# Making the low parts of the expert weights on VectorE instead of GpSimd

## The chip, the cores and the metric

One core of a Trainium2 chip runs the whole program. The metric is the device time of one execution in microseconds (us); the time before is the median of 3 runs.

## The reference, cut to what matters

Attention over 4 x 8 heads gives 2304 rows of 512 features; a gated MLP with RMS norm follows; then the part that matters here, a mixture of 8 experts with a fixed capacity:

```python
cap = N // E                                  # 2304 / 8 = 288
logits = x @ w_gate
order = np.argsort(-logits.flatten())
for idx in order:                             # greedy, best pair of token and expert first
    tok, e = (int(idx) // E, int(idx) % E)
    if assigned[tok] >= 0 or counts[e] >= cap:
        continue
    assigned[tok] = e
    counts[e] += 1
for e in range(E):
    mask = assigned == e
    h = np.maximum(x[mask] @ w1[e], 0.0)      # 288x512 by 512x1024
    out[mask] = h @ w2[e]                     # 288x1024 by 1024x512
```

## The kernel before, in words

The first 880 us are attention and the gated MLP, which the change does not touch. The rest is the function `routed`.

**Products.** Every fp32 operand is kept as a high part, rounded to the format that TensorE multiplies at full rate, and a low part, the difference. A product is three matmuls (`mm3`, lines 1029 to 1033): high by high, high by low, low by high. An expert has 16 units of 12 matmuls, each with 288 columns: `ffn1` eight times (one block of 128 hidden features each), then `ffn2` eight times (four output blocks, two halves each). After a unit, ScalarE takes the high part out of PSUM (lines 1044, 1023) and VectorE the low part (lines 1045, 1024). Four transposes at the start bring an expert's gathered tokens into place (`xpose`), four at the end turn its outputs (`turn`), and GpSimd's indirect DMAs gather and scatter the rows.

**Weights.** An expert's weights come in 8 slots of 128x1024 (512 KB each), loaded by SyncE's queue as soon as the expert is known and one of 8 buffers is free (`load`, `weights`). `split` (lines 1007 to 1013) makes of a slot the two parts: ScalarE copies it into the high part `wh`, and GpSimd subtracts that from the slot, which gives the low part `wl`. A slot serves two units. `cut` emits the splits so that they are LOOK = 4 slots ahead of the unit that is being emitted.

**Routing.** It closes one expert per phase. In a phase (`propose`, `search`, `close`) VectorE finds each token's best open expert (lines 788 to 798), and a search in six steps finds the threshold: VectorE makes candidates (`ci`, line 834), compares all tokens with them (`g`, line 801, two comparisons of half of the tokens each), TensorE counts with 18 small matmuls (line 807), VectorE tests the counts (`sat`, line 853), one matmul spreads the result (line 856) and VectorE scans it (line 861). Then come prefix sums (line 897 and the matmuls of lines 908 and 909) and a chain of 18-column operations. `tokens` turns the result into row numbers (the table `hb`, line 965; 18 matmuls, line 977) and starts the gather. Phase 0 runs before the first expert's products, the others beside the products; phase r + 1 starts only when the tokens of expert r - 1 are transposed (the loop on `turned` in `phases`, line 1105).

**Order of the work.** Every engine runs its instructions in the order in which they are emitted, and that order is laid out by hand. Two clocks are kept while emitting: `now` for TensorE and `vec` for VectorE. After each matmul of a product, `aside` adds 0.12 us to `now` and emits the operations of the routing whose time has come by these clocks. A flow hands over the cost of its next operation on either engine before it goes on. VectorE work that has some time is put in the list `late` by `evac`, with a weight (0.37 us by default) and a due time WAIT = 0.8 us after `now`. It leaves the list first in, first out, when it is due or when it fits ahead of the routing's next operation (by up to FIT = 0.4 us), and then `vec` is advanced by its weight; `settle` empties the list as far as a tag demands. `ffn1` and `ffn2` call `settle` with the slot's tag `(r, s)` before they use a slot (lines 1038 and 1052); in the kernel before, nothing in the list carries such a tag. GpSimd's subtraction is emitted directly after ScalarE's copy and is in neither clock.

Of the kernel before, what the change touches and what calls it, by code (L numbers as in the profile page):

```python
# [38 lines left out]
def body(tc, kq, vv, tab, w64, rg, wg2, w1, w2, ident_d, tri_d, jtab_d, cand_d, itab_d, out, dbg=None):  # L39
# [11 lines left out]
    wg2_t = cst.tile([128, 4, NE], F32, name="wg2_t")  # L51
    # the identity between the router's blocks (hi and lo, hi beside it)
    WI = cst.tile([128, 2, 160], F32R, name="WI")
# [4 lines left out]

    # ------------------------------------------------------------------ attention and MoE 1
    st = ExitStack()  # L60
# [72 lines left out]
    def rope_mul(n):  # L133
        """k and q turned: x cos + (x swapped) sin."""
        dve.tensor_mul(X[n][:, 0], X[n][:, 0], tab_t[:, 0])
        pool.tensor_mul(X[n][:, 1], X[n][:, 1], tab_t[:, 1])
# [30 lines left out]
    def v_scale(n):  # L167
        """A power of two that brings the head's V into the range of the halves."""
        p = VA.pop(n)
        sc = IS[n] = wa.tile([128, 3], I32, name="sc", bufs=3)  # L170
        dve.tensor_scalar(sc[:, 0:1], p[:, 0:1].bitcast(I32), 0x7F800000, None, op0=ALU.bitwise_and)
        dve.tensor_scalar(sc[:, 2:3], sc[:, 0:1], float(27 << 23), float(-(14 << 23)), op0=ALU.max, op1=ALU.add)
        dve.tensor_scalar(sc[:, 1:2], sc[:, 2:3], -1.0, float(254 << 23), op0=ALU.mult, op1=ALU.add)
# [107 lines left out]
    def step(u):  # L281
        """One step: scores of tile u, maxima of a tile ahead, the product with V of a tile behind,
        and its share of what the heads around need. Each engine finds its operands made a step or
        more before, so that none holds up another."""
        n, kt = divmod(u, KT)
# [78 lines left out]

    # ---- RMS norm and the transposed input
    def prep(b):
# [7 lines left out]
        def stats():  # L374
            """The squares of the last head; those of the others are there."""
            dve.tensor_scalar(m, m, 1.0 / DM, 1e-6, op0=ALU.mult, op1=ALU.add)
            for t in range(KT):
                squares(t, DM - D, DM, c)
# [39 lines left out]

    # ---- weights of MoE 1 in slots of 4 blocks
    NSLOT = 2 * NF + 12  # L420
# [4 lines left out]
    def w_ahead(to):  # L425
        """Loads the slots up to one, which there is room for."""
        while w_next[0] <= to and w_next[0] < B * NSLOT:
            n = w_next[0]
            w_next[0] += 1
            if n < NSLOT:  # L430
                if n < 2 * NF and n % 3 == 2:
                    WR[n] = flat[:, 0:1024].bitcast(I32).rearrange("p (k c w) -> p k c w", k=4, w=2)
                else:
                    WR[n] = wk.tile([128, 4, 128, 2], I32, name="w8")
                sp.dma_start(WR[n], w64[n].bitcast(I32))
            else:
                WR[n] = wk.tile([128, 4, 128], F32, name="wr" if n % 2 else "w8")
                sp.dma_start(WR[n], ws[n % NSLOT])
# [4 lines left out]
    def w_turn(g):  # L443
        """Queues the making of float32 words from the bits of slot g, and their store for later use."""
        if g >= NSLOT:
# [24 lines left out]
    def w_split(g):  # L470
        """Queues what brings slot g in its two parts, and the words of the slot after the next."""
        if g >= B * NSLOT:
# [33 lines left out]
    def pump():  # L506
        """Splits the slots that take the room of those used up to the unit before."""
        while used and used[0][0] < unit[0]:
            w_split(used.pop(0)[1] + NW)
        unit[0] += 1  # L510
        drain(2 if queue and queue[0][0] < NSLOT else 3)
# [32 lines left out]
    def logits(b, d, hf):  # L544
        """A block of features: turned into rows, and its part of the router's logits beside."""
        xh, xl = XT.pop((b, d, hf))
        j = 2 * (b % 2) + hf
        t0 = b // 2 * 9
        p = psB.tile([128, 512], F32, name="pb")
        # the last 32 rows go to partitions 32 j on, behind rows that nobody reads  # L550
        cut = [(0, 0, 128), (1, 128, 128), (2, 256 - 32 * j, 32 * j + 32)]
# [160 lines left out]
def routed(tc, top, t1, w1, w2, tri_d, jtab_d, cand_d, itab_d, out):  # L712
    """Each phase closes one expert: the one whose CAP-th best proposal is the best of such. A
    token proposes to the open expert it likes best; the expert closed takes its CAP best
    proposals, and the others propose anew."""
    nc = tc.nc
# [31 lines left out]
    dve.memset(taken, BIG)  # L748
    # row 8 of a satisfied table is 1: lift's product is 2^120 or more where an expert is
    # satisfied, -2^120 elsewhere  # L750
    lift = c2.tile([NE + 1, 128], BF16, name="lift")
    dve.tensor_scalar(lift, itab[0:NE + 1, 30:31].to_broadcast([NE + 1, 128]), 2.0 ** 120, None, op0=ALU.mult)
    # the sum of the marks of the satisfied experts
    marks = c2.tile([NE + 1, 128], BF16, name="marks")
# [16 lines left out]

    # The routing is written as flows: before each of its operations it hands over what that
    # will cost on the tensor and on the vector engine (us), and goes on when its time has come.

    HT = NT // 2

    # a token's proposal: v its value, wm the mark of the expert, 2^(8 - expert)
    def propose(r, lo=0, hi=NT):
# [33 lines left out]
    def early():  # L812
        """Half of the first phase's first step."""
        for _ in propose(0, 0, HT):
            pass
        g, p = R[0]["first"] = grid()
        compare(0, g, cand0, 0, 64)
        yield
        count(0, g, p, 0, 64)

    def search(r):
        """The largest value that some expert has CAP proposals at or above, a few bits at a
        time; the candidates are in falling order."""
        z = R[r]
        v = z["v"]
        o = 0
        for s, (_, bits) in enumerate(STEPS):
# [34 lines left out]
            fp = y[:, n - 1:n]  # L862
        # of the experts that have them, the first
        f = z["f"] = wk.tile([128, 2, NT], BF16, name="f")
# [11 lines left out]
    def last(r):  # L876
        """The expert that is left takes the tokens that are left."""
        z = R[r]
# [7 lines left out]
    def close(r):  # L886
# [25 lines left out]
        yield 0, 0.08  # L912
        # how many of those at the threshold there is room for
        dve.tensor_scalar(k[:, 2:3], q[:, 0, NT:], -1.0, float(CAP), op0=ALU.mult, op1=ALU.add)
# [26 lines left out]
    def tokens(r):  # L941
        """From a closed expert to its tokens' rows."""
        z = R.pop(r)
# [14 lines left out]
        dve.scalar_tensor_tensor(bb, ai, float(-GT), pos, op0=ALU.mult, op1=ALU.add)  # L958
        # two tiles side by side: 16-bit pairs go through at twice the rate
        hb = wk.tile([128, HT, GT, 2], BF16, name="hb")  # L960
# [26 lines left out]
        if r == 0:  # L987
            # the rest of the first weights comes behind these rows
            e = wk.tile([1, 1], I32, name="ev2")
            pool.tensor_copy(e, evs[0])  # L990
            sv[0] = sp.value_load(e, min_val=0, max_val=NE - 1)
            held.clear()
            load()
# [13 lines left out]
    def split(r, s):  # L1007
# [3 lines left out]
        act.activation(h, t, AF.Copy)  # L1011
        pool.tensor_sub(l, t, h.bitcast(F32))  # L1012
        ws[r, s] = (h, l)
# [69 lines left out]

    # The order of the emission: the experts' products one after the other, and between them,
    # when its operands are about to be there, the next operation of the routing; for that, the
    # clocks of the two engines are kept as they will run.
    now, vec = [1.1], [0.0]
# [23 lines left out]
    def hum(t):  # L1111
        """The array would fall back to half its clock while nothing but the routing runs."""
        while cold and t - now[0] > 0.4:
# [41 lines left out]
    def evac(tag, f, w=0.37):  # L1155
        """A vector operation that has some time."""
        late.append((now[0] + WAIT, w, f, tag))
# [7 lines left out]
    def settle(tag, keep=0):  # L1165
        """No more than the last few of a kind are still to come."""
        while sum(x[3] == tag for x in late) > keep:
            flush(1)

    def load():  # L1170
        """Weights of known experts, as far as there is room."""
        while loads and loads[0][0] in known and len(loads) > len(splits) - 8 and loads[0][1] not in held:
# [48 lines left out]
def rows():  # L1221
    """The row of each place of the router's tiles: of the half of a batch two tiles of 128 and a
    quarter of the ninth."""
    p, t = np.arange(128)[:, None], np.arange(NT)[None]
# [75 lines left out]
```

## Time and profile before

| what | value |
|---|---|
| time, median of 3 runs (lowest, highest) | 1280.33 us (1279.73, 1283.87) |
| span of the profiled execution (its only own time) | 1273.8 us |
| TensorE, VectorE, ScalarE, GpSimd busy | 1112.7, 803.8, 601.2, 772.9 us |
| mean granted TensorE clock | 0.939 |

The span runs from the first to the last instruction of one execution that the profiler recorded; a run's time is some 6.5 us longer. In the rows, PE is TensorE, PEld its weight loads, DVE VectorE, ACT ScalarE, POOL GpSimd, SP SyncE. A line reads: line of the kernel, engine, operation, output<-inputs, shapes. In a timeline the first two numbers are start and duration in us, and brackets hold the engine's idle time ahead of the instruction and what ended it.

### The profile page before, as it was taken

Reading aid. Unit: us, or ns where it says so; the run is one execution under the profiler, and the core shown is the slowest. Engines: PE = TensorE matmul, PEld = TensorE weight load, DVE = VectorE, ACT = ScalarE, POOL = GpSimd, SP = SyncE. Lnnn points to the kernel's source line nnn. Section 1 sums busy time; section 2 is a strip of 40 time slices with the busy share of each in tenths; the row PEclk is TensorE's granted clock in tenths of the full one; section 3 lists DMA queues with packets and bytes.
Section 4 is the critical chain, followed back from the end, with each engine's and each line's share of the span. In section 5 each row is a group of like instructions: output and inputs, shape, how many; then the busy total and the mean of one; then the engine's idle time right before and its main releaser. Section 6 shows DMA issues by size and latency. Waiting matters only on the chain.

```text
span 1273.8 us, 25985 instructions
## 1 busy us (share of the span) xinstructions
PE 1112.7 (87%) x9973; PEld 1033.8 (81%) x9973; DVE 803.8 (63%) x1825; ACT 601.2 (47%) x1387; POOL 772.9 (61%) x623
## 2 busy tenths in 40 slices
PE   3677789888979999888999999999888778988997
PEld 2666678787979999878999999997477767777996
DVE  6799889889885566456655343222776778567320
ACT  3566755445555656455665554432032233233552
POOL 4687678888546888534776526641254454455874
PEclk9897798999999999888999999999998889799999
DMA  5766446556653536334341223220322433343531
GB/s 167 190 179 176 129 139 201 192 160 179 192 152 107 155 94 176 81 97 135 93 127 57 78 80 105 84 81 25 114 105 103 152 130 92 103 129 115 178 112 32
DMA packets 73196, 159.04 MB, mean 125 GB/s; under 512 B 8976, under 2 KB 22960, under 8 KB 73072
## 3 DMA queue, kind: packets, MB, share of 16 engines
q1 hardware_dynamic: 70000, 147.94, 38.9%
q0 software_dynamic: 3072, 9.44, 2.5%
q8 instruction: 78, 1.28, 0.4%
q14 instruction: 46, 0.38, 0.1%
HBM read 110.52 MB, written 18.87 MB: 102 GB/s over the span
## 4 chain that ended last, share of the span: by engine, by line
PE 57%; DVE 26%; issue 5%; DMA 4%; ACT 3%; POOL 3%; SPq 1%; another core or an unknown queue 0%; POOLq 0%; DVEq 0%; ACTq 0%
PE psf L1032 13%; PE pb L500 9%; PE pb L501 9%; PE pb L502 9%; DVE mx L215 3%; DVE wr L459 2%; PE pss L807 2%; PE pa L190 2%; PE pa L208 2%; DVE wr L455 2%; DVE ci L834 2%; DMA QQ<-X 2%; PE pa L191 2%; DVE g L801 2%; DVE L L571 1%
## 5 line engine op out<-in xcount | busy, mean ns | idle before, releaser
L500 PE MATMUL pb<-XH,wh 128*128 128x288 f32 x768 | 230.2, 300 | 1.9 <-DVE t L532 1.9
L501 PE MATMUL pb<-XL,wh 128*128 128x288 f32 x768 | 229.4, 299 | 0.0
L502 PE MATMUL pb<-XH,wl 128*128 128x288 f32 x768 | 229.4, 299 | 0.0
L1012 POOL TENSOR_TENSOR wl<-rw,wh 128x1024 fp32r<-128x1024 f32 x64 | 153.5, 2410 | 104.2 <-ACT wh L1011 101.8
L202 POOL TENSOR_TENSOR PL<-pe,PH 128x576 f16<-128x576 f32 x136 | 189.2, 1396 | 37.4 <-ACT PH L199 26.8
L196 ACT ACTIVATE pe<-pa 128x288 f32<-128x288 f32 x320 | 121.7, 409 | 126.2 <-PE pa L191 118.5
L482 POOL TENSOR_TENSOR wl<-wr,wh 128x512 fp32r<-128x512 f32 x90 | 118.8, 1320 | 98.5 <-ACT wh L481 98.2
L500 PEld LDWEIGHTS pb<-XH,wh 128*128 128x128 f32 x768 | 147.8, 192 | 2.2 <-DVE t L532 2.1
L501 PEld LDWEIGHTS pb<-XL,wh 128*128 128x128 f32 x768 | 147.4, 192 | 0.0
L502 PEld LDWEIGHTS pb<-XH,wl 128*128 128x128 f32 x768 | 147.2, 192 | 0.0
L538 POOL TENSOR_TENSOR HL<-q,HH 128x288 fp32r<-128x288 f32 x96 | 87.2, 909 | 85.1 <-ACT HH L537 80.3
L190 PE MATMUL pa<-QQ,KK 128*128 128x288 f32 x320 | 107.9, 338 | 13.1 <-DVE mx L215 10.1
L500 PE MATMUL pb<-HH,wh 128*128 128x288 f32 x384 | 117.0, 305 | 0.7 <-DVE XL L402 0.5
L208 PE MATMUL pa<-KK,QQ 128*128 128x288 f32 x230 | 83.3, 362 | 36.9 <-ACT pe L196 22.3
L502 PE MATMUL pb<-HH,wl 128*128 128x288 f32 x384 | 114.3, 298 | 1.3 <-POOL wl L482 1.3
L501 PE MATMUL pb<-HL,wh 128*128 128x288 f32 x384 | 114.2, 297 | 0.0
L215 DVE TENSOR_REDUCE mx<-pa 128x1 f32<-128x288 f32 x230 | 101.3, 449 | 13.2 <-PE pa L208 12.8
L199 ACT ACTIVATE PH<-pe 128x576 f16<-128x576 f32 x160 | 108.8, 680 | 0.0
L532 DVE SCALAR_TENSOR_TENSOR t<-t,pb 128x288 f32<-128x288 f32 x96 | 43.5, 453 | 102.5 <-ACT t L531 101.8
L191 PE MATMUL pa<-QQ,KK 128*128 128x288 f32 x320 | 101.5, 318 | 1.8 <-DMA QQ<-mt 1.8
L482 POOL TENSOR_TENSOR wl<-w,wh 128x512 fp32r<-128x512 f32 x54 | 69.8, 1293 | 45.0 <-ACT wh L481 44.9
L481 ACT ACTIVATE wh<-wr 128x512 fp32r<-128x512 f32 x90 | 56.3, 625 | 72.0 <-DVE wr L459 65.8
(209 smaller groups left out, 3350.1 us busy)
## 6 DMA issues: line engine op xcount, KB each, us to landing
rw<-w SPq DMA_DIRECT2D x64, 512.0 KB
X<-kq SPq DMA_DIRECT2D x31, 576.0 KB
w<-w SPq DMA_DIRECT2D x28, 512.0 KB
w<-ws SPq DMA_DIRECT2D x54, 256.0 KB
wr<-ws SPq DMA_DIRECT2D x54, 256.0 KB
ws<-wr SPq DMA_DIRECT2D x36, 256.0 KB
KK<-X SPq DMA_DIRECT2D x31, 288.0 KB
QQ<-X SPq DMA_DIRECT2D x31, 288.0 KB
```

The costliest lines, as they stand in the source:

```text
L190: pe.matmul(p[:, 0:HS], BK[i][:, ks], AQ[i][:, qs], start=True, stop=False)
L191: pe.matmul(p[:, 0:HS], FK[i][:, ks], EQ[i][:, qs], start=False, stop=True)
L196: act.activation(E[u][:, h * HS:(h + 1) * HS], SM.pop((u, h))[:, 0:HS], AF.Exp, scale=1.0 / math.sqrt(D))
L199: act.activation(PH[u % NP][:, 0:S], E[u], AF.Copy)
L202: eng.tensor_sub(PL[u % NP][:, 0:S], E.pop(u), PH[u % NP][:, 0:S])
L215: dve.tensor_reduce(MX[n][:, qt, h:h + 1], XM.pop((u, h))[:, 0:HS], axis=AX.X, op=ALU.max)
L482: pool.tensor_sub(l, r, h.bitcast(F32))
L500: pe.matmul(p, wh[:, k], xh, start=first, stop=False)
L501: pe.matmul(p, wh[:, k], xl, start=False, stop=False)
L502: pe.matmul(p, wl[:, k], xh, start=False, stop=last)
L1012: pool.tensor_sub(l, t, h.bitcast(F32))
L1032: pe.matmul(p, a[:, k], b, start=first and i == 0, stop=last and i == 2)
```

## The change

In `split`, the subtraction that makes `wl` goes from GpSimd to VectorE, and from direct emission into the list `late`, with the tag `(r, s)` and the weight 1.13 us. It holds for all 64 slots. The rest of the diff takes comments and docstrings out.

```diff
@@ -1009,7 +1009,7 @@
         h = wb.tile([128, 8, 128], F32R, name="wh", bufs=8)
         l = wb.tile([128, 8, 128], F32R, name="wl", bufs=8)
         act.activation(h, t, AF.Copy)
-        pool.tensor_sub(l, t, h.bitcast(F32))
+        evac((r, s), lambda: dve.tensor_sub(l, t, h.bitcast(F32)), 1.13)
         ws[r, s] = (h, l)
```

## Rows read from the trace of the kernel before

**Rows 1.** The page: its first line.

```profile
span 1273.8 us, 25985 instructions
```

**Rows 2.** Windows, one per expert's products (us: length, busy time of each engine, clock, DMA).

```profile
core 0: us, PE busy (x) PEld busy (x) DVE busy (x) ACT busy (x) POOL busy (x), PEclk, DMA share, GB/s
924.80:978.80 54.00, 44.01 (x407) 39.62 (x406) 39.00 (x96) 17.18 (x29) 27.36 (x14) 0.89 0.28 102
978.80:1031.00 52.20, 43.30 (x378) 38.69 (x376) 37.44 (x108) 15.17 (x27) 23.09 (x16) 0.87 0.30 104
1031.00:1086.90 55.90, 43.98 (x392) 39.81 (x390) 44.02 (x110) 16.10 (x29) 28.50 (x19) 0.88 0.42 135
1086.90:1134.20 47.30, 42.24 (x371) 38.00 (x371) 31.14 (x85) 15.90 (x28) 25.83 (x20) 0.89 0.38 115
1134.20:1179.20 45.00, 36.35 (x317) 33.75 (x317) 31.85 (x97) 15.81 (x28) 24.04 (x17) 0.96 0.39 121
1179.20:1208.60 29.40, 29.01 (x236) 28.82 (x236) 9.24 (x20) 15.58 (x29) 25.11 (x17) 1.00 0.52 167
1208.60:1236.60 28.00, 28.00 (x218) 27.97 (x217) 5.49 (x12) 15.70 (x29) 22.04 (x14) 1.00 0.43 134
1236.60:1263.70 27.10, 27.09 (x206) 26.83 (x204) 3.67 (x8) 10.64 (x21) 14.85 (x12) 1.00 0.08 23
```

**Rows 3.** Waits of the stretch 913 to 1184 us.

```profile
PE pss L807 <- DVE g L801: 24.7, 17, 3.2
...
DVE hl L1045 <- ACT hh L1044: 13.3, 14, 2.6
```

**Rows 4.** Timeline of DVE and POOL (start us, us): three of the stretched operations.

```profile
915.34 5.21 DVE L834 TENSOR_TENSOR ci<-jtab,y 128x64 int32<-128x64 int32 x1
...
915.82 4.64 POOL L1012 TENSOR_TENSOR wl<-rw,wh 128x1024 fp32r<-128x1024 f32 x2
...
943.42 2.38 POOL L1012 TENSOR_TENSOR wl<-rw,wh 128x1024 fp32r<-128x1024 f32 x1 [3.15 <-ACT wh L1011]
...
943.47 2.37 DVE L872 TENSOR_SCALAR f<-v,y 128x18 bf16<-128x18 f32 x1
...
1178.86 3.40 DVE L965 TENSOR_TENSOR hb<-bb,pb 128x576 bf16<-128x576 bf16 x3
...
1179.28 2.66 POOL L1012 TENSOR_TENSOR wl<-rw,wh 128x1024 fp32r<-128x1024 f32 x1 [3.07 <-ACT wh L1011]
```

**Rows 5.** Lines: durations min/median/max in ns.

```profile
L872 DVE TENSOR_SCALAR f<-v,y x7: 228/231/2369, 902.7 to 1151.2; 128x18 bf16<-128x18 f32 x7
...
L1045 DVE SCALAR_TENSOR_TENSOR hl<-psf,hh x64: 435/458/460, 928.5 to 1250.4; 128x288 fp32r<-128x288 f32 x64
```

**Rows 6.** The page's costliest groups: the subtraction that the change moves.

```profile
L1012 POOL TENSOR_TENSOR wl<-rw,wh 128x1024 fp32r<-128x1024 f32 x64 | 153.5, 2410 | 104.2 <-ACT wh L1011 101.8
```

**Rows 7.** Timeline of PE: a wait in the first window ahead of expert 0.

```profile
921.39 0.64 PE L807 MATMUL pss<-g,oh 128*8 128x64 bf16 x9 [3.18 <-DVE g L801]
```

**Rows 8.** Timeline of DVE: pairs of comparisons, 128x576 and 128x288.

```profile
912.20 1.43 DVE L801 TENSOR_TENSOR g<-v,cand 128x576 bf16<-128x576 f32 x2
...
936.21 0.83 DVE L801 TENSOR_TENSOR g<-v,ci 128x288 bf16<-128x288 f32 x2
```

**Rows 9.** Lines of ScalarE: what comes ahead of the subtraction.

```profile
L1011 ACT ACTIVATE wh<-rw x64: 1043/1051/1063, 909.5 to 1248.6; 128x1024 fp32r<-128x1024 f32 x64
...
L1044 ACT ACTIVATE hh<-psf x64: 402/412/414, 928.1 to 1249.9; 128x288 fp32r<-128x288 f32 x64
```

**Rows 10.** Timeline of PE: a wait in a stretch at full clock.

```profile
1142.86 0.17 PE L856 MATMUL pss<-sat,lift 9*128 9x32 bf16 x1 [2.00 <-DVE sat L853]
```

**Rows 11.** Windows: the stretch with that wait (columns as in rows 2).

```profile
1120.00:1160.00 40.00, 34.09 (x330) 30.79 (x331) 28.44 (x80) 14.31 (x26) 22.62 (x16) 1.00 0.41 122
```

**Rows 12.** Timeline of DVE: where phases 1 and 5 begin.

```profile
910.42 0.29 DVE L788 TENSOR_REDUCE v<-L 128x18 f32<-128x144 f32 x1
...
1073.77 0.30 DVE L788 TENSOR_REDUCE v<-L 128x18 f32<-128x144 f32 x1
```

## The prediction, made before the changed kernel was run

> **What bounds the kernel now.** I began with the page's first line for the span [rows 1], then took the windows cut at the experts' first matmuls, because the change touches nothing ahead of them. There experts 0 to 4, whose products run with the routing between them, take 54.0, 52.2, 55.9, 47.3 and 45.0 us, 254.4 in all; experts 6 and 7, which run alone, take 28.0 and 27.1 [rows 2]. The reader should see that the same 192 products cost nearly twice as much beside the routing, and that TensorE is not busy for it: its busy time in the five windows adds up to 209.9 us, so it stands still for 44.5, and its granted clock is 0.87 to 0.96 instead of 1.00 [rows 2].
>
> Next, what TensorE waits for. The chain of waits names VectorE: the counting matmuls alone wait 24.7 us for the comparisons [rows 3]. So I read the timeline of VectorE for why it is late. An 18-column operation of 0.23 us takes 2.37 us; it ends at 945.84, where GpSimd's subtraction of a low part, begun 0.05 us earlier, ends at 945.80 [rows 4, 5]. The first such case, 5.21 us, ends with two subtractions in a row, and a later one lies in three table comparisons that take 3.40 us together [rows 4]. In the stretch 913 to 1184 us I count 40 operations of VectorE that run over the shortest of their own form by more than 0.15 us, 70.4 us over in all; each of them lies against one of the 44 subtractions that GpSimd makes there (line 1012, 2.41 us each [rows 6]). Operations that read PSUM are never stretched: the 64 on line 1045 take 435 to 460 ns [rows 5]. Of TensorE's standing still in the five windows, all but some 4 us falls in or right behind a stretched operation. So 40.5 us of idle TensorE come from 63.2 us of stretch (70.4 without the first case, 5.0, and the last, 2.2, which lie outside the windows): 0.64 us of idle for each us that VectorE is late without the emission's clocks knowing.
>
> **The change, part by part.** (a) *Removed: the stretches.* GpSimd keeps only gathers, scatters and 1-element fills at this stage, so the 40.5 us of idle go, and, ahead of expert 0, most of a 3.18 us wait [rows 7] in which the two first subtractions blocked a candidate table; two of them on VectorE still take 2.3 us there, partly under the gather, so I count -2.
>
> (b) *Added: 64 subtractions on VectorE.* No row shows this shape there. Two comparisons of 576 columns take 1.43 us and two of 288 take 0.83 [rows 8]; a second one costs some 0.68 and 0.38, so 1024 columns occupy VectorE for 0.68 + 448 x 0.30/288 = 1.14 us. The Trainium skill (VectorE: DVE Perf Modes, "The DRAIN you can't avoid") says that the next operation starts only when the pipe is empty, which would make it the full duration, about 1.21 us, and 49 of them 3 us dearer on the engine; the pairs here, shorter than two single ones, speak for 1.14. VectorE is busy for 183.4 us of the five windows [rows 2]; without 63.2 and with 41 x 1.14 = 46.7 that is 167 us, so there is room, though little within a phase.
>
> The planned 1.14 itself costs TensorE nothing in my sum: the operation is queued with a weight of 1.13 us on VectorE's clock, so what follows in the routing is emitted later and more of the expert's matmuls are put in front of it. These are the cover; if they run out, the phase becomes the bound (first rival).
>
> (c) *Added: a wait.* The subtraction needs ScalarE's high part (1.05 us), which is emitted at the start of a unit behind the last unit's evacuation (0.41 us) [rows 9]. On GpSimd that wait held up nothing. On VectorE the comparisons and prefix operations queued behind it wait too, and TensorE for them, and the emission's clock doesn't know of it. Bounds: 0, where VectorE comes late itself; at most 0.41 + 1.05 = 1.46 us. The nearest row is line 1045, which waits for the same evacuation one step earlier: 13.3 us over the 41 in the stretch [rows 3], 0.32 each. The new one needs ScalarE for 1.05 more, of which its neighbour's 0.45 and routing operations cover part. I take 0.7. As experts get shorter and phases don't, one more expert's 8 subtractions fall among the routing: 41 + 8 = 49. So 49 x 0.7 x 0.64 = 22 us of new idle.
>
> (d) *The clock.* Clock times length leaves 5.9 + 6.8 + 6.7 + 5.2 + 1.8 = 26.4 us of full-speed time lost in the five windows; TensorE was busy for 0.825 of it, so 21.8 us could return. A wait of 2.00 us stands in a stretch granted 1.00, the 2.4 GHz level [rows 10, 11], and the new waits should be under 1.5. I take three quarters back, -16; bounds 0 and -21.8.
>
> (e) *Queues.* On GpSimd's queue, gathers and scatters no longer stand behind a subtraction of up to 2.7 us; no gather decides an expert's start often, so 0. On SyncE's, loads wait for a buffer until the subtraction has read it; it is made 4 pairs of units before its use, as before, and the loads have nothing else behind them: 0. ScalarE's work is unchanged. Experts 6 and 7 [rows 2] and the tail up to the span's end don't change: VectorE is nearly idle there.
>
> Sum: -40.5 + 22 - 16 - 2 = -36.5 us. The profiled execution gives only its span, 1273.8 [rows 1]; the median of the runs is 1280.3, so 6.5 us lie around it and stay. 1273.8 - 36.5 + 6.5 = 1243.8, say **1244 us**.
>
> A second way: phases 1 to 4 take (1073.77 - 910.42)/4 = 40.8 us [rows 12], of which 8 x 63.2/41 = 12.3 is stretch, so 28.5 are left, and 8 subtractions at 1.14 + 0.7 make 43.2. Six experts at that pace from 924.8 on, then 28.0 + 27.1 + 10.1 of tail: 1249 us of span, 1256 of time, if nothing of the subtractions falls into VectorE's own waits. The two agree well enough, and tell that the routing phase is close to being the bound.
>
> **Rivals.** *VectorE's queue becomes the bound* (slower). Each subtraction waits the full 1.46 us at the head of VectorE's queue: a phase is then 28.5 + 8 x 2.6 = 49.3 us, every expert up to the sixth waits for its own phase, and the span is 924.8 + 6 x 49.3 + 65.2 = 1285.8, the time **1292 us**. It decides from a phase of 47.3 us on, that is from a mean wait of 1.2 us. For it: TensorE, held by a late comparison, ends its unit late, so that ScalarE is late and VectorE waits once more. Against it: line 1045 waits so little [rows 3], and a VectorE that is late already finds its operand there. Chance 0.16.
>
> *The clock stays down* (less gain). Short waits after every subtraction keep TensorE at its lower level: no -16, **1260 us**. For it: the clock is below 1.00 in all five windows with routing; against it [rows 10, 11]. Chance 0.12. The Trainium skill (TensorE: Matmul & The Clock Gate, "A second HAM failure mode: psum-queue depth-cycling") tells of a kernel whose many very short pauses between groups of matmuls make the clock swing; by that rule it would be this case, while the stretch at 1.00 with several short waits speaks against it here.
>
> *VectorE is never waited for.* The wait of (c) is 0, and the clock returns whole: -40.5 - 21.8 - 2, **1216 us**. The planner's slack would have to cover everything. Chance 0.12.
>
> *Nothing comes of it.* Low parts pile up in the list and are flushed only when a unit needs them; TensorE then waits for each instead of for a comparison, about the 0.9 us per subtraction that it loses now: 1280. Against it: they are due 0.8 us after they are queued. Chance 0.06.
>
> **How the numbers follow.** My own case, 1225 to 1255 around 1244, has 0.54. What a measurement here tells from no change is 0.3%, 4 us. Faster by more: 0.54 + 0.12 + 0.12 = 0.78; same 0.06; slower 0.16. The low end is the case without any new wait, 1216. Upward the bound of (c), 49 x 1.46 x 0.64 = 46 us of idle, would give 1268 with the clock back; I go to 1274, which leaves out most of the slower rival and half of the case of no change, under 2 in 10.
>
> **What would show it.** In the changed profile, line 1012 stands on VectorE at about 1.2 us; the 18-column operation of line 872 has a maximum near its median of 231 ns; the waits of counting matmuls for comparisons fall from 24.7 us to some 12; VectorE shows a new wait for line 1011 of some 30 us in all; the windows of experts 0 to 4 are 42 to 46 us long at a clock of 0.95 or more, and routing reaches into expert 5. I am wrong if stretches of 2 us remain without GpSimd's subtractions, if VectorE waits over 60 us for line 1011, or if the experts' windows stay near 50 us.

## The result, and the profile after

The changed kernel takes 1243.8 us (median of 4 runs, 1242.5 to 1246.9) beside 1280.8 us of the kernel before (4 runs): ratio 0.971, 95% interval 0.969 to 0.974, 37 us faster. Its profiled execution took 1242.45 us for a span of 1240.7, so only 1.75 us lie around a span. If that holds for the kernel before too, its profiled execution was a quick one, near 1275.5 us, and most of the 6.5 us that the prediction put around its span is the spread of its runs.

The page after, span and busy time of each engine. GpSimd has lost the 64 subtractions, and VectorE's total has not grown by them:

```profile
span 1240.7 us, 25976 instructions
...
PE 1106.4 (89%) x9973; PEld 1029.9 (83%) x9973; DVE 802.4 (65%) x1889; ACT 603.5 (49%) x1387; POOL 624.3 (50%) x559
```

The line of the subtraction (durations min/median/max in ns) and what VectorE waited for in front of it (us, times):

```profile
L1012 DVE TENSOR_TENSOR wl<-rw,wh x64: 1214/1225/1228, 914.7 to 1216.6; 128x1024 fp32r<-128x1024 f32 x64
...
  ACT wh L1011: 32.3, 44
```

The 18-column operation of line 872, which had a maximum of 2369 ns [rows 5]:

```profile
L872 DVE TENSOR_SCALAR f<-v,y x7: 227/229/232, 900.5 to 1142.0; 128x18 bf16<-128x18 f32 x7
```

No operation of VectorE in the routing is over the shortest of its form by more than 0.15 us any more; the 70.4 us are gone, and 64 subtractions of 1.22 us and 32.3 us of waiting for ScalarE have come. In the timeline of VectorE a comparison starts 1.14 us after a subtraction, as the pairs of [rows 8] said:

```profile
926.38 1.22 DVE L1012 TENSOR_TENSOR wl<-rw,wh 128x1024 fp32r<-128x1024 f32 x1 [0.49 <-ACT wh L1011]
927.52 0.45 DVE L801 TENSOR_TENSOR g<-v,ci 128x288 bf16<-128x288 f32 x1
```

The windows of TensorE are what surprises. Here they are cut at the first and last product of an expert, so that the lines of 21.80, 6.80, 4.80 and 8.30 us are gaps between two experts (columns as in [rows 2]; experts 3 and 4 are like expert 2 and left out):

```profile
918.40:951.30 32.90, 32.87 (x284) 30.61 (x282) 21.36 (x67) 12.23 (x22) 0.00 (x0) 0.96 0.25 98
951.30:973.10 21.80, 8.75 (x106) 7.05 (x107) 14.95 (x36) 5.76 (x8) 3.21 (x4) 0.59 0.51 186
973.10:1007.70 34.60, 34.60 (x322) 32.28 (x321) 26.49 (x81) 14.50 (x24) 6.54 (x8) 0.96 0.41 147
1007.70:1014.50 6.80, 4.42 (x52) 3.10 (x51) 4.50 (x15) 2.06 (x5) 1.32 (x2) 0.65 0.16 52
1014.50:1050.00 35.50, 35.50 (x307) 32.92 (x305) 26.41 (x81) 14.05 (x23) 6.41 (x9) 0.92 0.42 149
1050.00:1054.80 4.80, 3.19 (x52) 2.62 (x51) 3.65 (x11) 1.53 (x4) 0.00 (x0) 0.93 0.10 32
...
1133.90:1165.90 32.00, 31.95 (x248) 30.70 (x248) 23.46 (x89) 14.47 (x24) 5.78 (x7) 0.91 0.56 202
1165.90:1174.20 8.30, 3.20 (x30) 2.55 (x30) 2.77 (x8) 1.38 (x4) 4.39 (x6) 0.76 0.65 185
1174.20:1203.60 29.40, 29.40 (x219) 29.38 (x219) 14.44 (x21) 15.97 (x29) 3.60 (x6) 0.95 0.31 97
1203.60:1230.60 27.00, 27.00 (x205) 26.75 (x204) 9.43 (x13) 10.61 (x20) 3.60 (x6) 1.00 0.08 22
```

Within an expert TensorE no longer stands still at all: 32.9 us of 32.9, 34.6 of 34.6. It stands still between experts instead, most of all ahead of expert 1. From start to start the first six experts take 54.7, 41.3, 40.3, 39.5, 39.6 and 40.3 us. Over the whole stretch of the products, first the kernel before, then the changed one:

```profile
924.80:1263.70 338.90, 293.98 (x2507) 273.49 (x2506) 201.86 (x530) 122.08 (x217) 190.82 (x126) 0.92 0.35 114
```

```profile
918.40:1230.60 312.20, 286.71 (x2509) 267.36 (x2507) 206.32 (x593) 124.59 (x218) 47.25 (x64) 0.91 0.37 130
```

The stretch is 26.7 us shorter: idle time (length less busy time) fell from 44.9 to 25.5 us, and the busy time of the same matmuls by 7.3 us. The rest of the difference of the spans, 6.4 us, lies ahead of the first expert, which starts at 918.4 instead of 924.8.

The gap ahead of expert 1 can be read in three timelines of the changed kernel. ScalarE's copies of expert 1's first four slots each wait for their load (the bracket), since expert 1 became known only just before (SyncE issues its loads from 947.98 on):

```profile
951.48 1.06 ACT L1011 ACTIVATE wh<-rw 128x1024 fp32r<-128x1024 f32 x1 [1.27 <-DMA rw<-w]
952.71 1.06 ACT L1011 ACTIVATE wh<-rw 128x1024 fp32r<-128x1024 f32 x1 [0.18 <-DMA rw<-w]
954.69 1.06 ACT L1011 ACTIVATE wh<-rw 128x1024 fp32r<-128x1024 f32 x1 [0.92 <-DMA rw<-w]
956.05 1.06 ACT L1011 ACTIVATE wh<-rw 128x1024 fp32r<-128x1024 f32 x1 [0.30 <-DMA rw<-w]
```

VectorE stands at the head of its queue with the four subtractions, and behind them the table `hb` of expert 1's own tokens:

```profile
952.56 2.46 DVE L1012 TENSOR_TENSOR wl<-rw,wh 128x1024 fp32r<-128x1024 f32 x2 [2.40 <-ACT wh L1011]
955.78 2.59 DVE L1012 TENSOR_TENSOR wl<-rw,wh 128x1024 fp32r<-128x1024 f32 x2 [0.76 <-ACT wh L1011]
...
958.50 0.45 DVE L965 TENSOR_TENSOR hb<-bb,pb 128x576 bf16<-128x576 bf16 x1
```

and TensorE for the comparisons of the next phase, which also stand there:

```profile
960.13 0.64 PE L807 MATMUL pss<-g,oh 128*8 128x64 bf16 x9 [8.86 <-DVE g L801]
```

VectorE's operation ahead of the four ends at 950.17 and the one behind them starts at 958.28, so they hold it for some 8 of the 21.8 us of the gap. The rest of the gap is the table, the gather and the transposes.

In the waits of the stretch 913 to 1184 us (us in total, times, longest), that one wait is 8.9 of the 14.2 us that counting matmuls wait for comparisons, 24.7 before [rows 3]:

```profile
DVE wl L1012 <- ACT wh L1011: 23.5, 34, 2.4
...
PE pss L807 <- DVE g L801: 14.2, 7, 8.9
```

One more number, for the experiments. I call **the routing** the time from the start of phase 1's first reduction (line 788) to the start of the last operation that makes row numbers (line 982). It began at 910.42 before [rows 12] and ended here:

```profile
1184.41 0.16 DVE L982 SCALAR_TENSOR_TENSOR ix<-ixf 96x3 int32<-96x3 f32 x1
```

After the change:

```profile
908.29 0.29 DVE L788 TENSOR_REDUCE v<-L 128x18 f32<-128x144 f32 x1
...
1168.69 0.16 DVE L982 SCALAR_TENSOR_TENSOR ix<-ixf 96x3 int32<-96x3 f32 x1
```

274.0 us became 260.4.

### The profile page after: what moved, and what is told of

It is laid out like the page before. It is cut to its first block, busy times and chain, and to the rows that moved or that the text cites. A ratio compares the mean times of both kernels' runs of the same rounds, so it can differ in the third digit from the quotient of the medians.

```text
span 1240.7 us, 25976 instructions
## 1 busy us (share of the span) xinstructions
PE 1106.4 (89%) x9973; PEld 1029.9 (83%) x9973; DVE 802.4 (65%) x1889; ACT 603.5 (49%) x1387; POOL 624.3 (50%) x559
## 4 chain that ended last, share of the span: by engine, by line
PE 61%; DVE 21%; DMA 6%; issue 4%; ACT 3%; POOL 3%; SPq 1%; POOLq 0%; DVEq 0%; ACTq 0%
PE psf L1032 17%; PE pb L500 9%; PE pb L502 9%; PE pb L501 9%; DVE mx L215 4%; DVE wr L455 2%; DVE wr L459 2%; PE pa L190 2%; PE pa L208 2%; DVE L L571 2%; PE pss L807 2%; DMA QQ<-X 2%; PE pa L191 1%; DVE X L135 1%; PE psf L1114 1%
## 5 line engine op out<-in xcount | busy, mean ns | idle before, releaser
L985 POOL DMA_INDIRECT gx<-xs,ix x24 | 25.6, 1065 | 211.5 <-PE psf L1032 66.1
L215 DVE TENSOR_REDUCE mx<-pa 128x1 f32<-128x288 f32 x230 | 101.2, 448 | 13.4 <-PE pa L208 12.9
L1012 DVE TENSOR_TENSOR wl<-rw,wh 128x1024 fp32r<-128x1024 f32 x64 | 78.2, 1224 | 32.8 <-ACT wh L1011 32.3
```

What stands on the lines that cost most here:

```text
L215: dve.tensor_reduce(MX[n][:, qt, h:h + 1], XM.pop((u, h))[:, 0:HS], axis=AX.X, op=ALU.max)
```

## The experiments

Three things came with the change: another engine, the list that delays the subtraction, and the weight by which VectorE's clock counts it. The first four runs take them apart. Theory A is the prediction's: TensorE loses what the emission's clocks don't know.

**The engine alone.** The subtraction goes to VectorE, but is emitted right behind the copy:

```diff
-        evac((r, s), lambda: dve.tensor_sub(l, t, h.bitcast(F32)), 1.13)
+        dve.tensor_sub(l, t, h.bitcast(F32))
```

> VectorE subtracts directly behind ScalarE's copy in the emission, outside the list and its clock. Theory A (what the emission's clocks do not know is what costs TensorE): each of some 45 subtractions holds VectorE for 1.14 us and a wait of 1.0 to 1.4, all of it unplanned, 2.3 us x 45 x 0.64 = 66 us of idle inside the experts against 40 of the kernel before, so 1290 to 1310 us. Rival B (only how long VectorE is occupied matters, planned or not): the wait grows by some 0.5 us per subtraction, 1244 + 49 x 0.5 x 0.64 = 1255 to 1265 us.

Measured: 0.995 of the kernel before (0.992 to 0.998), 1276 us. The waits for ScalarE in front of the subtraction doubled (changed kernel: 32.3 us):

```profile
  ACT wh L1011: 67.1, 51
```

Neither theory had the size. What it says about the change is plain: moving the work to VectorE alone is worth 0.5%; the list makes the difference, as the next run shows.

**The list without the weight.**

```diff
-        evac((r, s), lambda: dve.tensor_sub(l, t, h.bitcast(F32)), 1.13)
+        evac((r, s), lambda: dve.tensor_sub(l, t, h.bitcast(F32)), 0.0)
```

> As the changed kernel, but with the weight 0 instead of 1.13 us, so that the list still delays the subtraction and VectorE's clock does not count it. Theory A: 1.14 + 0.7 us unplanned per subtraction, against 1.6 of the kernel before; 49 x 1.84 x 0.64 = 58 us of idle, 1275 to 1295 us. Rival B: within 6 us of the changed kernel, 1238 to 1250 us.

Measured: 0.964 (0.959 to 0.968), 1236 us: faster than the changed kernel, and a little under rival B's range. Theory A falls here, since nothing of the subtraction is in a clock any more. TensorE does stand still within the experts again (21.5 us, 0.4 between them), and the waits for VectorE are many and short (us, times, longest):

```profile
PE pss L856 <- DVE sat L853: 9.9, 13, 1.8
...
PE pss L807 <- DVE g L801: 5.1, 9, 1.6
```

**The list and the weight, on GpSimd.**

```diff
-        evac((r, s), lambda: dve.tensor_sub(l, t, h.bitcast(F32)), 1.13)
+        evac((r, s), lambda: pool.tensor_sub(l, t, h.bitcast(F32)), 1.13)
```

> As the changed kernel, list and weight included, but the subtraction runs on GpSimd again, so the stretches come back, some 40 of 1 to 2.2 us. Theory A: of 1.6 us of stretch per subtraction 1.13 is planned for, some 0.5 is not; idle inside the experts falls to 10 to 20 us, phases stay at 40 us and set the pace: 1240 to 1258 us, close to the changed kernel. Rival B (the shared time of the two engines is what costs): close to the kernel before, 1270 to 1285 us.

Measured: 0.995 (0.992 to 0.997), 1277 us, as the rival said. The stretches are back; the line of the candidates' table (median and maximum):

```profile
L834 DVE TENSOR_TENSOR ci<-jtab,y x35: 181/193/5314, 890.9 to 1166.4; 128x32 int32<-128x32 int32 x28, 128x64 int32<-128x64 int32 x7
```

There are gaps between the experts here too, 21.3 us ahead of expert 1. That one has a cause of its own, which I can read but did not take out: the row numbers are ready at 963.83, but the list has put four subtractions ahead of the gather on GpSimd's queue, and it starts 7.7 us later (in all other runs it starts 0.3 us after them):

```profile
961.46 9.94 POOL L1012 TENSOR_TENSOR wl<-rw,wh 128x1024 fp32r<-128x1024 f32 x4 [18.25 <-ACT wh L1011]
971.55 1.28 POOL L985 DMA_INDIRECT gx<-xs,ix  x1 [0.15 <-issue]
```

All five profiles with the weight, those below included, have 25 to 27 us of idle TensorE between experts, and none without it has more than some 1 us: the gaps come with the weight. With the stretches there, the weight brings 0.5% at most; how much the late gather takes of it is open.

**No subtraction at all.**

```diff
-        l = wb.tile([128, 8, 128], F32R, name="wl", bufs=8)
         act.activation(h, t, AF.Copy)
-        evac((r, s), lambda: dve.tensor_sub(l, t, h.bitcast(F32)), 1.13)
-        ws[r, s] = (h, l)
+        ws[r, s] = (h, h)
```

> The subtraction is left out on every engine; the high part stands in for the low one in the third matmul, so the low parts of the expert weights are missing from the result. It bounds what any place of the subtraction can give. Theory A, with phases of 28 to 30 us without it: experts run at TensorE's own 33 to 35 us, 918 + 6 x 35 + 56 + 10 = 1194 us of span, 1195 to 1210 us. Rival B' (the gaps between experts are gathers and transposes, not VectorE's phase): gaps of 4 to 8 us stay, 1220 to 1235 us.

Measured: 0.939 (0.934 to 0.944), 1203 us, in theory A's range. The routing takes 201.5 us, its first four phases 28.7 to 29.7 each (28.5 was the prediction's figure for a phase without stretches). VectorE stands idle for 71 us in it, waiting for other engines: keep that number in mind. TensorE hardly waits here, 0.6 us over the whole stretch of the products:

```profile
922.00:1193.10 271.10, 270.47 (x2507) 254.39 (x2505) 138.05 (x530) 121.98 (x217) 43.13 (x64) 0.99 0.45 149
```

So this run is a floor that TensorE's own work sets, at a clock of 0.99.

**Theory C.** The six profiles so far (before, changed and these four) fit another reading. From the end of the routing to the end of the span there are 89.4 us in the kernel before, 91.7, 89.4 and 89.7 where the subtraction has no weight or is not there, and 72.0 and 71.8 where it has the weight 1.13: three or two experts' products are then left. So the routing's length sets the time, and theory C says that VectorE's queue sets the routing: what a hold on that queue costs depends on where it falls. A stretch only ever hits an operation that is ready to run; a subtraction in the list can lie where VectorE would wait for TensorE anyway.

Four more runs tested this. **Early splits of expert 1 held back**, against the gap of 21.8 us:

```diff
-            cut((u + 1) // 2 + LOOK)
+            cut(min((u + 1) // 2 + LOOK, 8) if r == 0 else (u + 1) // 2 + LOOK)
```

> As the changed kernel, but no slot of expert 1 is split while expert 0 runs, so that VectorE does not stand behind copies that wait for the loads of weights only just known. Theory C (what TensorE is paced by is the routing on VectorE's queue; a hold at the queue's head ahead of expert 1's table delays its gather): the gap of 21.9 us ahead of expert 1 falls to 12 to 15 us, later phases come earlier by as much, 1233 to 1239 us. Rival (the gap is the gather's own way and the planner's clock): the gap stays at 20 us or more, 1241 to 1248 us.

Measured: 0.981 (0.978 to 0.985), 1251 us on a chip where the kernel before takes 1273.8: slower than the changed kernel by ratio. Neither forecast held. The first gap fell to 16.8 us, but the next grew from 6.8 to 15.4. VectorE's timeline shows the same pattern moved on to expert 2, a queue head waiting for copies that come late:

```profile
1002.57 1.23 DVE L1012 TENSOR_TENSOR wl<-rw,wh 128x1024 fp32r<-128x1024 f32 x1 [3.02 <-ACT wh L1011]
...
1006.93 1.23 DVE L1012 TENSOR_TENSOR wl<-rw,wh 128x1024 fp32r<-128x1024 f32 x1 [1.21 <-ACT wh L1011]
...
1010.12 1.22 DVE L1012 TENSOR_TENSOR wl<-rw,wh 128x1024 fp32r<-128x1024 f32 x1
```

**Entry into the list when the copy is done**, by TensorE's clock, with weight 0:

```diff
-        evac((r, s), lambda: dve.tensor_sub(l, t, h.bitcast(F32)), 1.13)
+        pend.append((now[0] + 1.5, (r, s), lambda: dve.tensor_sub(l, t, h.bitcast(F32))))
...
+    def ripe(tag=None):
+        while pend and (pend[0][0] <= now[0] or any(x[1] == tag for x in pend)):
+            _, g, f = pend.pop(0)
+            evac(g, f, 0.0)
```

(`ripe` is called first thing in `aside` after the clock has moved, and in `settle` with its tag.)

> As the kernel with weight 0, but a subtraction enters the list only 1.5 us (on TensorE's clock) after its copy is emitted, when ScalarE should be done. Theory C (unhidden hold of VectorE's queue lengthens the routing, and the span is some 1000 us plus the routing): VectorE's wait for the copies falls from 30 us to under 10, the routing from 237 to 222 to 232 us, 1222 to 1232 us. Rival (those waits lie in time in which VectorE would wait for counts anyway): no change, 1233 to 1241 us.

Measured: 0.962 (0.959 to 0.965), 1224.8 us. The waits for ScalarE within the routing are gone (0.3 us of 12.9), and the routing is 223.9 us. All that is as theory C had it. But this chip is quicker than that of the runs before it, and by ratio the kernel is no better than the one with weight 0 (0.962 beside 0.964), so the comparison was made again below.

**Fills in place of the subtraction**, on GpSimd:

```diff
-        evac((r, s), lambda: dve.tensor_sub(l, t, h.bitcast(F32)), 1.13)
+        for _ in range(2):
+            pool.memset(l.bitcast(F32), 0.0)
```

> GpSimd keeps its part, but in place of the subtraction it fills the low part with zeros, twice; the low parts of the expert weights are missing from the result. The fills write SBUF and read nothing. Theory C with the shared read side as cause of the stretches: operations of VectorE with two SBUF operands are not stretched, and the routing is near that of the kernel without low parts, 1200 to 1215 us. Rival (any long GpSimd instruction blocks VectorE): 40 or so stretches as long as a fill, 1240 to 1280 us.

Measured: 0.947 (0.944 to 0.950), 1208 us; the routing is 208.1 us. GpSimd is nearly as long at work per slot (2 x 0.95 us), and hardly anything is stretched: 14 operations, 6.0 us in all. The lines of the fills, of two operations of VectorE with two tensor inputs in SBUF, and of two with one (min/median/max in ns):

```profile
L1013 POOL MEMSET wl<- x128: 941/954/997, 917.7 to 1184.8; 128x1024 f32 x128
...
L834 DVE TENSOR_TENSOR ci<-jtab,y x35: 181/192/261, 891.8 to 1089.8; 128x32 int32<-128x32 int32 x28, 128x64 int32<-128x64 int32 x7
...
L801 DVE TENSOR_TENSOR g<-v,ci x70: 449/457/759, 892.0 to 1090.4; 128x288 bf16<-128x288 f32 x56, 128x576 bf16<-128x576 f32 x14
L801 DVE TENSOR_TENSOR g<-v,cand x14: 744/754/762, 849.0 to 1072.5; 128x576 bf16<-128x576 f32 x14
...
L872 DVE TENSOR_SCALAR f<-v,y x7: 227/229/910, 904.1 to 1093.7; 128x18 bf16<-128x18 f32 x7
...
L949 DVE TENSOR_SCALAR ps<-acc x8: 166/170/722, 906.7 to 1113.4; 128x18 f32<-128x18 f32 x8
```

The candidates and comparisons (lines 834, 801) stay at their own durations. It is not that they missed the fills: 18 candidate tables, 36 comparisons and 5 more operations with two inputs (lines 965, 928) began while a fill ran, and none took over 0.02 us more than the shortest of its form. In the kernel before, 24 of these began while a subtraction ran, and all were held, for 0.18 to 2.24 us. Operations with one tensor input (872, 949), fp32 throughout or into bf16, are over by up to 0.7 us with the fills, line 869's by 0.9 us, and what is queued right behind them is late with them. So it is GpSimd's reading that blocks an operation with two inputs, and not its being busy.

**Both edits, weight kept.** The early splits of expert 1 held back, and the entry into the list when the copy is done, with `evac(g, f, 1.13)` in place of 0.0:

> As the changed kernel with weight 1.13, no early splits of expert 1, and the entry into the list 1.5 us after the copy. Theory C: both gains of the two separate edits, gaps between experts of 2 to 4 us after the first, phases of 36 to 38 us: 1218 to 1230 us. Rival (with the weight planned, the emission's clock holds the routing back whatever VectorE does): phases stay at 39 to 40 us, 1233 to 1242 us.

Measured: 0.982 (0.979 to 0.984), 1252 us: the rival, and above its range. VectorE waits for ScalarE's copies for 0.5 us within the routing, and still the routing takes 265.7 us, with 77.6 us in which VectorE stands idle for something else, against 45.7 in the run with the later entry and weight 0: it waits 17.8 us for the counting matmuls, 8.1 there. The run with held splits and the weight alone, on the same chip, took 1251.4 us, so with the weight the waits for ScalarE cost nothing that shows; and gaps of 16.2 and 11.9 us stay ahead of experts 1 and 2, so the head of VectorE's queue makes the smaller part of them. The weight itself holds the routing back. This run differs from the one with weight 0 by the held splits too; the clean pair, weight 1.13 against 0 alone, comes next.

The last four ran on one chip, where the kernel before takes 1280.8 us:

> The changed kernel unaltered, on the same chip as the next three. All theories: 0.971 of the kernel before.

> The kernel with weight 0 once more, beside the changed kernel. Theory C (the planned 1.13 us holds the routing's emission back and so gives part of the gain away): 6 to 10 us under the changed kernel. Rival (the two earlier results came from two chips and differ by no more than chips do): within 3 us of it.

> Weight 0 and entry into the list 1.5 us after the copy, beside the kernel with weight 0. Theory C: the routing is shorter by the waits for ScalarE that are gone (12.9 us in the profile of the kernel with weight 0, part of it hidden), 4 to 12 us under that kernel. Rival (those waits were hidden): within 2 us.

> As the one before, but each low part is made in two subtractions of 512 columns, some 0.62 us each, that enter the list one after the other. Theory C (a queued subtraction costs the routing what does not fit into VectorE's own waits): smaller pieces fit better, the routing is 4 to 10 us shorter, 3 to 8 us under the kernel with whole subtractions. Rival (the sum of the work counts): 45 more fixed costs of some 0.07 us, 0 to 4 us over it.

The last one's edit:

```diff
-        pend.append((now[0] + 1.5, (r, s), lambda: dve.tensor_sub(l, t, h.bitcast(F32))))
+        for i in (slice(0, 4), slice(4, 8)):
+            pend.append((now[0] + 1.5, (r, s), lambda i=i: dve.tensor_sub(l[:, i], t[:, i], h[:, i].bitcast(F32))))
```

| kernel | us | ratio to before (95%) |
|---|---|---|
| changed | 1246.1 | 0.972 (0.969 to 0.975) |
| weight 0 | 1237.4 | 0.966 (0.963 to 0.969) |
| weight 0, entry when the copy is done | 1215.9 | 0.947 (0.944 to 0.951) |
| the same, in two halves | 1219.5 | 0.952 (0.949 to 0.955) |

Weight 0 is 9 us under the changed kernel, as theory C had it, and its routing takes 235.9 us beside 261.3. The later entry gives 21 us more, over its 4 to 12. Halves are some 4 us slower, with intervals that overlap: the rival, and a limit of theory C, since smaller pieces do not fit better. The best kernel is the third, 65 us under the kernel before and 30 under the changed one.

The whole stretch of the products in the first three (weight 1.13, weight 0, weight 0 with the later entry) shows that these gains are not idle time alone:

```profile
923.60:1235.90 312.30, 286.80 (x2508) 267.35 (x2507) 206.58 (x593) 124.47 (x217) 46.41 (x64) 0.91 0.37 129
```

```profile
916.40:1221.30 304.90, 281.59 (x2508) 262.49 (x2506) 207.42 (x593) 122.17 (x217) 49.29 (x64) 0.96 0.41 132
```

```profile
924.80:1206.50 281.70, 272.45 (x2507) 254.57 (x2505) 207.11 (x594) 121.97 (x217) 47.21 (x64) 0.99 0.44 143
```

Without the weight the stretch is 7.4 us shorter: 5.2 are TensorE's busy time at a better clock, 2.2 its idle time. With the later entry it is 23.2 us shorter again, 9.1 of busy time and 14.1 of idle time; VectorE's waits for the copies, 12.6 us less, are only a part of that.

The same kernel with the later entry had a ratio of 0.962 on the other chip and 0.947 here, and a routing of 223.9 and 212.8 us. Why they differ so much I did not find. In both routings VectorE is busy for the same 178 us; it stands idle for 46.0 and 35.2. TensorE was granted a clock of 0.92 and 0.96 in experts 1 and 3 there, and 1.00 here. That goes with the longer waits; that it causes them was not tested.

The subtraction's line in the best kernel, and what VectorE waited for in front of it:

```profile
L1012 DVE TENSOR_TENSOR wl<-rw,wh x64: 1198/1218/1227, 924.9 to 1193.6; 128x1024 fp32r<-128x1024 f32 x64
...
  ACT wh L1011: 7.4, 5
```

The profiles in one table; of the changed kernel and of weight 0 it has the first profile. A hold is what the subtraction takes of VectorE's queue within the routing: the stretches, or the durations of the subtractions and VectorE's idle time in front of them.

| kernel | routing, us | hold, us | over no subtraction | per us of hold |
|---|---|---|---|---|
| GpSimd, weight 1.13 | 293.3 | 85.7 stretch | 91.8 | 1.07 |
| before | 274.0 | 70.4 stretch | 72.5 | 1.03 |
| VectorE, direct | 271.9 | 55.1 + 38.9 | 70.4 | 0.75 |
| changed, early splits held back | 267.4 | 63.6 + 21.5 | 65.9 | 0.77 |
| both edits, weight 1.13 | 265.7 | 62.0 + 0.5 | 64.2 | 1.03 |
| changed | 260.4 | 63.6 + 22.6 | 58.9 | 0.68 |
| weight 0 | 237.3 | 55.0 + 12.9 | 35.8 | 0.53 |
| weight 0, later entry (first time) | 223.9 | 54.6 + 0.3 | 22.4 | 0.41 |
| the same, in two halves (last chip) | 217.5 | 61.4 + 0.1 | 16.0 | 0.26 |
| weight 0, later entry (last chip) | 212.8 | 54.7 + 0.4 | 11.3 | 0.21 |
| fills | 208.1 | 6.0 stretch | 6.6 | 1.10 |
| no subtraction | 201.5 | 0 | 0 | |

The last column is a ratio and no price of a hold by itself: the weight and the granted clock differ between the rows as well. The two rows with held splits show it: with the weight, 22.6 us less of hold make the routing 1.7 us shorter.

## Why the prediction was right or wrong, point by point

The time came out as forecast, 1243.8 beside 1244, and the faster sign with it. That it agrees to 0.2 us is luck: the terms below are off by up to 9 us and cancel, the 6.5 us that it put around the span are 1.75 in the changed kernel, and one reason was wrong.

(a) *The stretches go.* Right, and shown twice: they vanish when GpSimd stops reading (in the changed kernel all, with the fills those of operations with two inputs), and come back when it reads again under the very same list and weight. The Trainium skill (SBUF — State Buffer, "Who interferes with whom") says that an operation of VectorE with two SBUF inputs collides with a GpSimd instruction that reads SBUF, not with one that only writes it, and that VectorE's modes with two ports contend with GpSimd, where it makes no such distinction. The fills agree: at most 261 ns on line 834, against 5205 before, and 722 and 910 on the one-input lines 949 and 872; in which mode those two lines ran, no row shows.

(b) *1.14 us on VectorE, free because it is planned for.* The size was right: the next operation starts 1.14 us after a subtraction of 1.22. The reason was wrong. Without the weight the kernel is 9 us faster, and with the weight on GpSimd only 0.5% is gained. The factor 0.64 us of idle per unplanned us described the kernel before and nothing else: in the changed kernel TensorE does not stand still within an expert at all, and the idle time went to the gaps, since the experts now follow the routing's phases. The prediction's net of idle, -40.5 + 22 = -18.5 us, measured -19.4, is right by luck: the idle time that is left lies between the experts and comes with the weight, not within them from the wait of (c).

(c) *The wait for ScalarE.* Predicted 0.7 us each over 49; within the routing 22.6 us over 52, 0.43 each. The upper bound of 1.46 us was wrong: one wait is 2.40, since ScalarE's copy itself stands behind the load of a slot that has only just been asked for, which the sum left out. With these waits gone and no weight 21 us are won, more than their size, but the edit also moves the subtractions to other places and TensorE's clock rises with it, so not all of that is theirs.

(d) *The clock.* Predicted -16; the busy time of the same matmuls fell by 7.3. The windows show why: it drops to 0.59 and 0.65 in the gaps and is 0.91 to 0.96 in the experts behind them: the long waits did not go, they moved. Where they are gone, in the best kernel, it is 0.99.

(e) *Queues and head.* -2 predicted ahead of expert 0, -6.4 measured, of which 2.1 lie ahead of the routing already (910.42 to 908.29) and are none of the change. No gather is delayed on GpSimd's queue, as forecast: each starts within 1.1 us of its row numbers. On VectorE's queue one is: ahead of expert 1 the table of its tokens waits some 8 us behind four subtractions whose slots are still being loaded. The prediction had looked at that wait for the units' own rhythm only.

Sum of the spans: -19.4 - 7.3 - 6.4 = -33.1, where -36.5 was forecast; the other 4 us of the medians' 37 would be the quick profiled execution of before.

The second way, by phases, was the better model: experts do follow the phases, which take (1148.81 - 908.29)/6 = 40.1 us, not 43.2, and the routing does reach past expert 5. Of the rivals, VectorE's queue as the bound was right as a mechanism, in that the phases pace the experts, and wrong in price: the phase would have had to take 47.3 us. The clock that stays down was half right. The signs named at the end held for line 872, for the wait for line 1011 (32.3 us, some 30 forecast) and for the comparisons (14.2, some 12), and not for a clock of 0.95 nor for windows of 42 to 46 us: from start to start the first expert takes 54.7 and the next four 39.5 to 41.3.

That a queued subtraction hides in VectorE's own waits is read from the table and from those waits (71 us without a subtraction, 48 in the changed kernel, 35 in the best), not forced by one experiment; the two halves speak against the simplest form of it, and with the weight, taking VectorE's waits for ScalarE away gained nothing.

## What to carry to other kernels

Where a chain of small VectorE operations paces a kernel, look for ones that take ten times their usual time and lay them beside GpSimd's instructions: in the two kernels that have such holds, the routing was longer by 1.03 and 1.07 us for each us of them. Where the work goes on the other engine's queue decides what moving it is worth: put directly behind its producer it gave 0.5%, in the list 3 to 4%, and entered when its operand was there 4 to 5%. Once TensorE hardly waits any more (9 us in the best kernel), there is little left to win by it. Test a planner's weight by setting it to zero before trusting it.

## What the runs showed that I had not expected

The weight that tells VectorE's clock the truth makes the kernel slower by 9 us (1246.1 against 1237.4). And two kernels of nearly one time, weight 0 and weight 1.13, have their idle time in quite different places: 21.5 us within the experts and 0.4 between them, at a clock of 0.95, or 0.0 and 25.4, at 0.91. That clock is most of the difference between them, 5.2 of 7.4 us where both ran on one chip. And the collision has another side: GpSimd's issue of an indirect DMA, 0.92 us undisturbed, took 1.83 us beside a subtraction on VectorE that had begun 0.2 us earlier. That is no single case: in the changed kernel nine issues that began beside a subtraction took 1.14 to 1.83 us, and each ended some 0.8 us after the subtraction did. What it costs was not tested.
